# Threshold attention with a bilinear ffn: the transposes of a unit and the writes of its blocks moved behind the slot's first ffn portion

## The chip, the cores and the metric

The kernel runs on one core of a Trainium2 chip. The metric is the device time of one execution in microseconds (us), of which the median of three runs is given. All data is fp32 on the engines; the ffn weights come as 8-byte floats and are converted on the chip.

The engines are named as the profile names them: PE is TensorE (PEld its weight loads), DVE is VectorE, ACT is ScalarE, POOL is GpSimd, SP is SyncE, which here issues nearly all DMAs. Each engine works through its own queue in order; an instruction that waits holds all that stand behind it.

## What is computed

```python
# batch 8, heads 8, seq 576, head_dim 64; d_model 512, d_ff 1536
scores = scale * q @ k.T                       # for each batch and head
thresh = scores.max(-1) - tau
scores = where(scores >= thresh, scores, -1e9)
attn = exp(scores - scores.max(-1)); attn /= attn.sum(-1) + 1e-9
x = (attn @ v), heads side by side             # 4608 tokens x 512
out = ((x @ w_a) * (x @ w_b)) @ w_out
```

## The kernel before

**Units and slots.** Heads are taken in 32 pairs. The 576 query rows of a pair make four units of 128 rows and the 64 rows left over make, with those of the next pair, a fifth kind of unit; there are 144 units. The main loop (L1091) runs over slots g. In a slot a unit passes its first stage, and units before it pass later ones:

- `scores` (L389): PE multiplies q and k into two PSUM tiles of 128x576 (L404); DVE takes the row maxima (L411, two of them) and subtracts the threshold (L412, thr).
- `weigh` (L422): ACT forms the exponentials into a tile tw (L431, L432); DVE puts the threshold on them and sums the rows (L435, two of them). After that the score tiles are free.
- `reciprocal` and `normalise`: DVE inverts the sums (L446, L448) and ACT scales the tile tw (L454).
- one slot later, `turn_blocks` (L497): DVE transposes the blocks of 32x32 in both halves of tw, in place (L502, two instructions of 128x576), and four DMAs write tw to a swap block in DRAM (posted at L515). There are three tw buffers.
- two slots later, `turn_back` (L517): DMAs read the swap block back as wT, now turned as a whole. It comes at the start of the slot, or behind the pv product if the slot has one, since there are two wT buffers.
- three slots later, for the second unit of a half, `weighted` (L610): PE multiplies wT and v (pv, L546), ACT and DVE copy the result out of PSUM into x tiles (L553, L554).

The first nine slots (g up to 8) turn their units on PE instead. So 136 of the 144 units pass `turn_blocks`.

**The ffn between.** When four head pairs of a batch have delivered a block of 256 tokens, the block goes to the ffn, a generator that issues PE work in steps. `advance(cols)` (L998) runs it for so many columns. A slot gives the ffn its share of columns (`pace`) in four portions, 0.3, 0.35, 0.15 and 0.2 of it: the first behind the scores (L1131), the second behind `weigh` (L1156), then pv, then `normalise`, then the last two (L1198). What belongs to the steps is issued with them: PE's matmuls (L724 and L828 for the first layer, L894 for the second), and the evictions from PSUM, by ACT (L773 to L785, L834, L535) and by DVE: L777 and L794 add a product to another, L789, L798 and L836 multiply or add into h, L536 adds the second half of a result onto ACT's copy. All PSUM tiles, those of scores, pv and ffn, come from one pool of four.

**The order.** Program order is kept on each engine: `keep_order` (L41) chains the instructions of an engine as the Python code issued them. So the place of a call in the loop is the place of its instructions in the queues.

**The DMAs.** `post` (L139) issues a DMA at once up to slot 36. From slot 37 on it puts it on a list, `bulk`; writes of tw and reads of wT are put ahead of other entries of this and the last slot. `passed` (L169), called for each ffn step, takes entries off the list: one of 36864 elements, as each of the four writes of a unit is, for every 320 columns. Each entry also waits for the PE instruction issued last before it. `flush` issues what must be there now.

In a slot the part around the change reads, in order: overdue DMAs; `turn_back` of unit g-2 if no pv comes; `scores` of unit g; on DVE the two maxima and thr; then `turn_blocks` of unit g-1 and the first ffn portion; then the transposes of q tiles that are due (`prep`, L365); then `weigh` of unit g.

Of the kernel before, what the change touches and what calls it, by code (L numbers as in the profile page):

```python
# [23 lines left out]
BY_PE = 8  # L24
# [9 lines left out]
PORTIONS = (0.3, 0.35, 0.15, 0.2)  # L34
# [20 lines left out]
def kernel(  # L55
# [113 lines left out]
    def passed(columns):  # L169

        running["pump"] += columns
        while bulk and running["pump"] >= 0:
            running["pump"] -= PUMP * sum(math.prod(to.shape) for to, _ in bulk[0][2]) // PART
            pump()
        if not bulk:
            running["pump"] = min(running["pump"], 0)
# [320 lines left out]
    def turn_blocks(i, u):  # L497

        ws, _ = weights.pop((i, u))
        t = whole.pop((i, u))  # L500
        for w in ws:
            nc.vector.transpose(w, w)  # L502
        swap = scratch.tile([G, P, NSLOT * Q], FP32, tag="swap" if u < NT else "swapt", name="swap")
        swaps[i, u] = swap
        for g in range(G):
            if u < NT:
                moves = [(swap[g].rearrange("(r p) e -> p r e", p=Q),
                          t[g * Q:(g + 1) * Q].rearrange("p (r s) e -> p r (s e)", r=G))]
            else:
                moves = []  # L510
                for m in range(2):
                    j = g // 2 ^ m
                    moves.append((swap[2 * m + g % 2, j * D:(j + 1) * D].rearrange("(r p) e -> p r e", p=Q),
                                  t[g * Q:(g + 1) * Q, m * NB:(m + 1) * NB].rearrange("p (r s) e -> p r (s e)", r=2)))
            post(("tw", i, u), *moves)  # L515
# [63 lines left out]
    def exchange_blocks():  # L579
        while complete and not state["layer"] and not blocks:  # L580
            x, what = complete.pop(0)
            xs, done = ahead.pop(what[1:], (None, 0)) if what[0] == "half" else (None, 0)
            xs = xs or x_tile("xS")
            for hp in range(done, HP):
                exchange(x, xs, hp, 0, HALF, nc.gpsimd)
            blocks.append(((x, xs) + ((x_sums(x), x_sums(xs)) if state["first"] >= 3 * SEVENS else ()), what))
        if not state["layer"] and not blocks:
            for key, count in settled.items():
                xs, done = ahead.get(key) or (x_tile("xS"), 0)
                for hp in range(done, count):  # L590
                    exchange(x_of[key], xs, hp, 0, HALF, nc.gpsimd)
                ahead[key] = xs, count
# [80 lines left out]
    def first_sums(n, group):  # L673

        quarter = [w[:, NG - 1 - group].rearrange("p (z y e) w -> p z y (e w)", z=2, y=2)[:, :, y]
                   for w in (wa_sb, wb_sb) for y in range(2)]
        s1, s2, s4 = (sums_at(group, m).rearrange("p (z w) -> p z w", z=2) for m in range(3))
        a11, a12, a21, a22 = quarter
        out, a, b, op = ((s1, a21, a22, ALU.add), (s2, s1, a11, ALU.subtract), (s4, a12, s2, ALU.subtract),
                         (a21, a11, a21, ALU.subtract))[n]  # L680
        nc.gpsimd.tensor_tensor(out, a, b, op=op)
# [310 lines left out]
    def cost():  # L992

        return BLOCK_COLS - (NF // 2 * CH if state["sums"] else 0) - (SEVENS * 2 * HP * P if state["first"] >= 3 * SEVENS else 0)
# [3 lines left out]
    def advance(cols):  # L998
        running["owed"] += cols
        while running["owed"] > 0:  # L1000
            if running["ffn"] is None:
                exchange_blocks()
                if not blocks:
                    running["owed"] = 0.0
                    return
                if len(blocks[0][0]) == 4 and state["first"] == 3 * SEVENS:
                    for group in range(SEVENS):
                        first_sums(3, group)
                    state["first"] += 1
                if state["over"] and not state["all"]:  # L1010
                    first_sums(3, SEVENS)
                    state["all"] = True
                running["tiles"] = len(blocks[0][0])
                running["ffn"] = ffn(*blocks.pop(0))
                running["left"] = cost()
            step, rest, whole = next(running["ffn"], (None, 0, 0))
            if step == 0:
                running["owed"] = 0.0
                return
            if step is None:  # L1020
                running["ffn"] = None
                state["through"] += 1
            else:
                running["owed"] -= step
                running["left"] -= step
                passed(step)
                running["done"] = running["done"] + step if rest else 0
                running["rest"] = rest
                running["room"] = min(ROOM, whole // 2)
# [19 lines left out]
    def backlog():  # L1049
        return (len(blocks) + len(complete)) * cost() + (running["left"] if running["ffn"] is not None else 0)  # L1050
# [40 lines left out]
    for g in range(len(units) + PV_LAG):  # L1091
# [20 lines left out]
        pace = (PACE if g > BY_PE else PACE_EARLY) * BLOCK_COLS  # L1112
        if g > BY_PE:
            pace = min(pace, backlog() / (min([a for a in arrivals if a > g] + [len(units) + PV_LAG + 1]) - g))
# [10 lines left out]
        if g == 3:  # L1125
            for c in range(0, NSUM - TURNED - 2 * CW + 1, 2 * CW):
                extra.append(sums_u32[:, c:c + 2 * CW].rearrange("p (f w) -> p f w", w=2))
        if g > BY_PE and g <= len(units):
            turn_blocks(*units[g - 1])
        if g > BY_PE:  # L1130
            advance(PORTIONS[0] * pace)  # L1131
        for p in range(HP, NPR):
            for name, d in (("q0", 1), ("q1", 1)):
                if g == (second if name == "q1" else first)[p] - d - (name == "q1" and p % 2):
# [120 lines left out]
```

## Time and profile before

| what | value |
|---|---|
| time, median of 3 runs | 1418.59 us (1414.69, 1418.59, 1419.03) |
| the profiled execution, device time | 1420.35 us |
| its span, first to last instruction | 1418.6 us |
| mean granted TensorE clock | 0.994 |
| PE busy | 1369.6 us, 33980 matmuls |
| DVE busy | 1017.8 us, 2212 instructions |
| ACT busy | 678.8 us, 1245 instructions |
| POOL busy | 492.6 us, 675 instructions |
| DMA | 223.21 MB, 157 GB/s over the span |
| swap<-tw, issue to landing (median) | 3.0 us |
| wT<-swap, issue to landing (median) | 3.7 us |

Busy times are unions of the instructions that the profiler recorded on an engine. The ends of matmuls are modelled, since they are pipelined. A row of a group names line, engine, operation, out and in with shapes, the count; then total busy time and the mean of one; then the idle time of the engine just before these instructions and what ended it. In the list of waits, `A <- B: x, n, y` says that A waited for B x us in all, n times, y at most. In a timeline the first two columns are start and duration in us; in square brackets stands the idle time before, with its releaser.

### The profile page before, as it was taken

What the parts mean: (1) busy time and instruction counts of PE and PEld (TensorE: products, weight loads), DVE (VectorE), ACT (ScalarE), POOL (GpSimd) and SP (SyncE); (2) the same over time, 40 slices, a digit from 0 to 9 for tenths busy, and PEclk for the clock granted to TensorE, in tenths of its full rate; (3) what the DMA queues carried; (4) which work ended last, traced back from release to release, by engine and by line L of the source; (5) the groups of instructions that cost most, each with busy time, mean ns of one, the idle gap of its engine ahead of it and who ended that gap; (6) DMA issues with size and microseconds to landing.
All of it is one profiled execution on the core that took longest, in us unless ns stands there. A gap on an engine that the chain in (4) does not pass through costs nothing.

```text
span 1418.6 us, 76564 instructions
## 1 busy us (share of the span) xinstructions
PE 1369.6 (97%) x33980; PEld 1240.7 (87%) x33980; DVE 1017.8 (72%) x2212; ACT 678.8 (48%) x1245; POOL 492.6 (35%) x675
## 2 busy tenths in 40 slices
PE   6879999999999999999999999999999999999998
PEld 4778589999879897978998999998898899799998
DVE  6998877787777877775767777677767776745425
ACT  5986545545445455544444545454545455431110
POOL 2774442415060606051324233241515060608100
PEclk9999999999999999999999999999999999999999
DMA  9976875667656775666556775567555775550000
GB/s 213 238 225 193 204 207 161 168 167 204 169 128 181 189 194 153 171 163 173 137 137 152 183 182 165 131 162 206 163 146 143 200 188 156 133 152 18 4 19 18
DMA packets 327449, 223.21 MB, mean 157 GB/s; under 512 B 171600, under 2 KB 311632, under 8 KB 327120
## 3 DMA queue, kind: packets, MB, share of 16 engines
q1 hardware_dynamic: 323936, 216.95, 58.9%
q8 instruction: 267, 4.37, 1.3%
q10 hardware_dynamic: 3184, 1.38, 0.4%
q14 instruction: 62, 0.51, 0.1%
HBM read 128.58 MB, written 89.65 MB: 154 GB/s over the span
## 4 chain that ended last, share of the span: by engine, by line
PE 84%; DVE 8%; DMA 5%; issue 2%; SPq 1%; ACT 0%; DVEq 0%; ACTq 0%
PE pab L724 28%; PE po L894 20%; PE pab L828 15%; PE sc L404 10%; PE pv L546 9%; DVE mx L411 2%; DVE tw L502 2%; DMA vm<-in_v_dram 1%; DMA wT<-swap 1%; DVE tw L435 1%; PE po L964 1%; DVE low L311 1%; DMA qT<-in_q_dram 1%; DVE u L794 1%; DMA more_u<-in_moe_w_a_dram 0%
## 5 line engine op out<-in xcount | busy, mean ns | idle before, releaser
L411 DVE TENSOR_REDUCE mx<-sc 128x1 f32<-128x576 f32 x288 | 204.6, 751 | 131.5 <-PE sc L404 131.1
L454 ACT ACTIVATE tw<-tw,rcp 128x576 f32<-128x576 f32 x272 | 196.0, 768 | 203.6 <-DVE rcp L448 203.6
L686 POOL TENSOR_TENSOR h<-h,u 128x512 f32<-128x512 f32 x28 | 35.1, 1275 | 607.2 <-DVE h L798 429.0
L432 ACT ACTIVATE tw<-sc,bias,scalars 128x576 f32<-128x576 f32 x288 | 239.3, 831 | 10.9 <-PE pab L828 0.4
L435 DVE SCALAR_TENSOR_TENSOR tw<-sc,thr,tw 128x576 f32<-128x576 f32 x288 | 221.2, 798 | 9.6 <-ACT tw L432 9.0
L894 PE MATMUL po<-wo_sb,h 64*64 64x256 f32 (+1 forms) x3408 | 205.6, 367 | 1.2 <-DVE h L798 1.1
L502 DVE STREAM_TRANSPOSE tw<-tw 128x576 f32<-128x576 f32 x272 | 194.3, 752 | 0.8 <-ACT tw L454 0.8
L894 PEld LDWEIGHTS po<-wo_sb,h 64*64 64x64 f32 x3408 | 156.9, 133 | 26.6 <-DVE h L798 2.6
L404 PE MATMUL sc<-kT,qT 64*64 64x288 f32 x2016 | 168.9, 404 | 2.3 <-issue 0.6
L546 PE MATMUL pv<-wT,vm 64*64 64x128 f32 (+3 forms) x5040 | 165.5, 274 | 3.3 <-issue 2.4
L546 PEld LDWEIGHTS pv<-wT,vm 64*64 64x64 f32 x5040 | 154.1, 134 | 13.8 <-issue 8.0
L857 POOL TENSOR_TENSOR h<-h 128x256 f32<-128x256 f32 x168 | 117.3, 731 | 107.5 <-PE po L894 97.3
L894 PE MATMUL po<-sums_u,h 64*64 64x256 f32 x2448 | 153.5, 376 | 0.7 <-DVE h L836 0.7
L724 PE MATMUL pab<-xU,wb_sb 64*64 64x128 f32 x4352 | 137.7, 269 | 0.0
L724 PEld LDWEIGHTS pab<-xU,wb_sb 64*64 64x64 f32 x4352 | 133.0, 133 | 2.6 <-issue 0.9
L894 PEld LDWEIGHTS po<-sums_u,h 64*64 64x64 f32 x2448 | 116.3, 133 | 20.7 <-DVE h L836 1.1
L404 PEld LDWEIGHTS sc<-kT,qT 64*64 64x64 f32 x2016 | 104.0, 133 | 22.1 <-issue 6.1
L431 ACT ACTIVATE bias<-mx,scalars 128x1 f32<-128x1 f32 x288 | 82.7, 287 | 67.1 <-DVE mx L411 66.5
L553 ACT COPY xT<-pv 128x128 f32<-128x128 f32 (+1 forms) x68 | 17.6, 258 | 200.6 <-PE pv L546 200.6
L554 DVE COPY xT<-pv 64x128 f32<-64x128 f32 (+1 forms) x136 | 38.2, 281 | 91.2 <-PE pv L546 89.8
L724 PE MATMUL pab<-xS,wa_sb 64*64 64x128 f32 x2176 | 101.2, 269 | 1.7 <-issue 1.6
L535 ACT COPY kept<-po 128x512 f32<-128x512 f32 x65 | 34.8, 535 | 123.1 <-PE po L894 109.3
(159 smaller groups left out, 2428.1 us busy)
## 6 DMA issues: line engine op xcount, KB each, us to landing
wT<-swap SPq DMA_DIRECT2D x242, 288.0 KB, 3.7
swap<-tw SPq DMA_DIRECT2D x480, 144.0 KB, 3.0
vm<-in_v_dram SPq DMA_DIRECT2D x128, 72.0 KB, 2.5
swap<-tw SPq DMA_DIRECT2D x128, 72.0 KB, 3.0
kT<-in_k_dram SPq DMA_DIRECT2D x112, 72.0 KB, 3.4
wT<-swap SPq DMA_DIRECT2D x56, 144.0 KB, 3.5
out_dram<-kept SPq DMA_DIRECT2D x27, 256.0 KB, 3.9
qT<-in_q_dram SPq DMA_DIRECT2D x112, 40.0 KB, 2.8
```

The lines of the kernel that those rows point to most:

```text
L404: nc.tensor.matmul(sc[m][o * D:o * D + wide, c], qT[r, q0:q0 + wide], kT[r, c * SH:(c + 1) * SH], start=True, stop=True)
L411: nc.vector.tensor_reduce(mx[:, c], sc[j], axis=AX.XY, op=ALU.max)
L431: nc.scalar.activation(bias[:, j:j + 1], mx[:, j:j + 1], AF.Copy, scale=e_nscale)
L432: nc.scalar.activation(wb[j], sb[j], AF.Exp, bias=bias[:, j:j + 1], scale=e_scale)
L435: nc.vector.scalar_tensor_tensor(out=wv, in0=sb[j], scalar=thr[:, j:j + 1], in1=wv, op0=ALU.is_ge, op1=ALU.mult, accum_out=sums[:, j:j + 1])
L454: nc.scalar.activation(w, w, AF.Copy, scale=rcp[:, j:j + 1])
L502: nc.vector.transpose(w, w)
L546: nc.tensor.matmul(pv[c * D:(c + 1) * D, y], vm[rows, s], wT[y](rows, s), start=(s == 0), stop=(s == NSLOT - 1))
L724: nc.tensor.matmul(out[c * D:(c + 1) * D, r, f * P:(f + 1) * P], w[g][k][rows, w0:w0 + D], moving[k][rows], start=(fresh and k == 0 and f ...
L828: nc.tensor.matmul(pab[c:c + columns(), r], w[rows, f // n, k, fs + c:fs + c + columns()], moving, start=(k == 0), stop=(k == H - 1))
L857: (nc.vector if state["over"] else nc.gpsimd).tensor_tensor(*a, **kw)
L894: nc.tensor.matmul(po[c * D:(c + 1) * D, r, y, cut], ht[rows, t0:t0 + D], other[rows, f, cut], start=(f == 0), stop=(f == NF // 2 - 1))
```

## The change

The call of `turn_blocks` for the last unit moves from ahead of the first portion to behind it. The guard of each call is the same as before, and no instruction is added or taken away.

```diff
@@ -1125,10 +1125,10 @@
         if g == 3:
             for c in range(0, NSUM - TURNED - 2 * CW + 1, 2 * CW):
                 extra.append(sums_u32[:, c:c + 2 * CW].rearrange("p (f w) -> p f w", w=2))
+        if g > BY_PE:
+            advance(PORTIONS[0] * pace)
         if g > BY_PE and g <= len(units):
             turn_blocks(*units[g - 1])
-        if g > BY_PE:
-            advance(PORTIONS[0] * pace)
         for p in range(HP, NPR):
             for name, d in (("q0", 1), ("q1", 1)):
                 if g == (second if name == "q1" else first)[p] - d - (name == "q1" and p % 2):
```

On DVE the two L502 of a unit then stand behind the evictions of the first portion, if it has any, and ahead of L365 and L435 as before. The four writes come onto the list when the first portion has been issued, so `passed` can offer them from the second portion on; up to slot 36 they are issued at that place.

## Prediction

> **What bounds the kernel now.** I read the busy shares first, then the chain that ended last, then the groups of VectorE, then the list of waits of TensorE (PE), and last the timeline of single slots. A slot is one turn of the main loop; there are 144 units and 136 of them are transposed by VectorE (DVE), two instructions each.
>
> ```profile
> PE 1369.6 (97%) x33980; PEld 1240.7 (87%) x33980; DVE 1017.8 (72%) x2212; ACT 678.8 (48%) x1245; POOL 492.6 (35%) x675
> ...
> PE 84%; DVE 8%; DMA 5%; issue 2%; SPq 1%; ACT 0%; DVEq 0%; ACTq 0%
> ...
> L502 DVE STREAM_TRANSPOSE tw<-tw 128x576 f32<-128x576 f32 x272 | 194.3, 752 | 0.8 <-ACT tw L454 0.8
> ```
>
> PE is busy nearly throughout and is 84% of the chain, so a change on DVE can only win or lose what PE waits for DVE. The moved instructions are L502: 752 ns each, and over 272 of them DVE stood idle just 0.8 us before one. Their input is always there when their turn comes; they cost their own length to whatever is queued behind them. Today that is the evictions of the first ffn portion, in those slots that have any. The waits of PE say whether that hurts:
>
> ```profile
> PE pab L828 <- DVE h L836: 2.5, 1, 2.5
> ...
> PE pab L724 <- DVE u L794: 1.6, 5, 0.4
> ...
> PE po L894 <- DVE h L798: 1.1, 2, 0.5
> PE pab L724 <- DVE kept L536: 0.8, 3, 0.3
> PE pv L546 <- DVE h L836: 0.8, 1, 0.8
> ...
> PE po L894 <- DVE h L836: 0.7, 1, 0.7
> ...
> PE pab L828 <- DVE osb L536: 0.4, 1, 0.4
> ```
>
> The columns are total us, times, longest. These are 14 waits of 7.9 us for an eviction on DVE. I looked each up in the timeline, and in all 14 the eviction stands directly behind the two transposes. One of them, the slot at 457 us, on DVE:
>
> ```profile
> 458.80 0.23 DVE L412 TENSOR_SCALAR thr<-mx,scalars 128x2 f32<-128x2 f32 x1
> 458.93 1.43 DVE L502 STREAM_TRANSPOSE tw<-tw 128x576 f32<-128x576 f32 x2
> 460.29 1.18 DVE L798 TENSOR_TENSOR h<-h,pab 128x1024 f32<-128x1024 f32 x1
> 461.39 0.80 DVE L435 SCALAR_TENSOR_TENSOR tw<-sc,thr,tw 128x576 f32<-128x576 f32 x1
> ```
>
> and on PE:
>
> ```profile
> 456.98 0.44 PE L724 MATMUL pab<-xS,first_u 64*64 64x128 f32 x5
> ...
> 458.92 2.06 PE L828 MATMUL pab<-xS,wb_sb 64*64 64x256 f32 x32
> 461.53 1.31 PE L894 MATMUL po<-wo_sb,h 64*64 64x256 f32 x20 [0.55 <-DVE h L798]
> ```
>
> The product that L798 evicts was complete at 457.5, DVE was through with thr at 459.0, yet the eviction began at 460.29, after 1.36 us of transposes; PE ran dry at 460.98 and went on at 461.53.
>
> **The change, part by part.** Nothing is added or removed. Three things move.
>
> 1. The order on DVE. It differs only where an instruction of the first portion lies between L502 and L435. Going through DVE's timeline slot by slot I count 45 such slots of 136; in the other 91 DVE's queue is word for word the same. In the 45, an eviction (L536 0.67, L836 0.67, L789, L777, L798 1.2, two L794 1.35 us) starts up to 1.36 us sooner, and the transposes end later by its length. L435, behind both, starts at the same time as long as the eviction's data is ready when thr ends.
>
> Gain. Each of the 14 waits is shorter than 1.36 us and goes whole, except the first (2.54 us at 106.6: L502 began at 104.83, L836 at 106.19, so 1.4 of it). That is 7.9 - 2.5 + 1.4 = 6.8 us as the lower end. It is too small: the matmul before the wait is drawn with 0.27 to 0.38 us although such matmuls follow each other every 0.03 to 0.05 us, so PE could have begun the next group some 0.25 us before the drawn end. The weight loads, which run just ahead of the matmuls, show the same waits as 2.7 (1 time), 4.2 (6), 2.6 (3), 2.2 (3), 1.6 (2), 1.1 (1), 1.0 (2) and 0.9 (1), together 16.3 us in 19 waits; less 1.3 for the first that is 15.0, the upper end. I take 6.8 + 14 x 0.25 = 10.3 and round it down to 9, since a wait that goes now and then uncovers a smaller one behind it. [...]
>
> Cost. Where the data is not ready, DVE now waits with the transposes behind it instead of doing them meanwhile, and L435 starts later by that wait. From PE's and ACT's timeline I find 14 of the 45 slots: mostly L536, which needs ACT's copy L535 (0.59 us) after the last matmul of po, 0.4 to 1.0 us each; the largest is the slot at 645 us:
>
> ```profile
> 647.26 1.43 DVE L502 STREAM_TRANSPOSE tw<-tw 128x576 f32<-128x576 f32 x2
> 649.78 1.22 DVE L777 TENSOR_TENSOR h<-h,pab 128x1024 f32<-128x1024 f32 x1 [1.10 <-PE pab L724]
> 650.92 0.81 DVE L435 SCALAR_TENSOR_TENSOR tw<-sc,thr,tw 128x576 f32<-128x576 f32 x1
> ```
>
> There L435 moves to about 652.4. Over the 14 slots the delays add to about 9.6 us. Behind L435 wait the two PSUM tiles of the scores, the reciprocal and ACT's normalisation. In the window from 200 to 1260 us no wait of PE is put down to L435, and DVE still has 89.8 us of idle time in front of the pv copies (L554) and 131.1 in front of L411 later in the slots; that is the cover. Without it the price is 9.6 us. I take 1, nearer to nothing because the rows for it are empty there.
>
> 2. The four writes of the swap block. They are posted behind the first portion, so SP's list offers them one portion later, some 1280 columns by the code; the chain shows 224 matmuls of L724 in 6.11 us and four of them make 128 columns, so this is 1.1 us. They cannot start before the transposes end, 3.2 us after the scores; by then the next portion is running, so for the 91 slots their issue time hardly moves. In the list of SP's own waits:
>
> ```profile
> SPq L157 <- DVE tw L502: 107.5, 54, 6.5
> ```
>
> 54 times SP stood at such a write for the transposes, with everything behind it held. Now loads and stores that are already in the list go first; that can only bring q, k and v earlier (DVE waits 6.3 us for q today). In the 45 slots the write is later by the eviction, up to 1.35 us. Reader of the block: wT, one slot later, then pv another slot later. Setting the landings of the wT reads against the start of their pv matmuls, I find 2.1 us or more to spare everywhere after slot 36, mostly 5 to 9. Up to slot 36, where spare time sinks to 0.6 us at 174, nothing is held in the list and SP's order stays the same. Cost 0; without the cover, each of 64 pv pieces could wait up to 1 us.
>
> 3. The tile of three tw buffers. It is written again three slots later, so a write that is 1 to 2 us late holds nobody. Cost 0. In the last slot with a transpose (at 1256 us) the first portion has no DVE instruction, so the end is as before.
>
> Sum: -9 + 1 = -8 us. The profiled execution took 1420.35 us for a span of 1418.6; on the span the result is 1410.6. The three runs have a median of 1418.59, 1.8 below the profiled one, and the same 8 us off it give **1410.6, say 1411**.
>
> **Rivals.**
>
> *Hidden anyway.* PE is one engine in a long chain; if it arrives sooner it may just wait for the next thing, ACT's copies or the issue waits (4.4 and 2.4 us in that window, which no DVE order touches). For it: total idle time of PE after 200 us is small. Against: the 14 waits are separate, 40 to 150 us apart mostly, with gap-free PE work in between, so there is nothing to catch up with. A quarter to nothing of the gain would be left: 1416 to 1419. On this side stands the Trainium skill, page "Perfetto Trace Analysis", section "Matmuls": groups should rotate through PSUM banks so that an eviction overlaps the next group's matmuls. By that rule a late eviction costs nothing and the time stays at 1418.6; the 14 rows above speak against it here, for PE wants exactly the tile or the h block that is still being evicted.
>
> *Scores late (slower).* DVE waits in order at an eviction whose product PE has not finished, and L435, with the score tiles and the next unit's whole softmax behind it, pays. Price now: 9.6 us in 14 slots, if PE pays all of it; with the lower gain 6.8 that is +2.8. It decides once more than 11.1 us reach PE, since 11.1 - 6.8 = 4.3. At 25 unready slots of 0.7 us it is 17.5 - 6.8 = +10.7, 1429. For it: PE and DVE share these slots closely and PE's timing shifts. Against: a PE that is less held up finishes products sooner relative to DVE, and no wait for L435 is seen now.
>
> *Not what it says.* In two thirds of the slots the order does not change; if the 14 waits came by another way than the order, the time stays within 2 us. I count this with the first.
>
> **Chances.** A time is told from no change here when it differs by about 0.3%, 4.3 us. Forecast 0.70, all of it faster by more; hidden anyway and not what it says 0.18, within; scores late 0.12, slower. The likeliest case runs from 1418.6 - 15.0 = 1404 to 1414. The range goes on to 1421, so that it holds the hidden case and leaves out little more than the slower one and what is below.
>
> **What would show it.** Right: the seven rows above are gone from PE's waits or below 2 us in sum; the slot of the 457 us example shows L798 directly behind L412 and L502 behind L798; L435 begins at an unchanged distance from L411 in most slots; PE's busy time is the same and the span shorter by the waits. Wrong: new rows of PE waiting for L435 or for wT of more than 3 us in sum, L554 idle time turned into PE waits, or the seven rows gone and the span unchanged.

## Result and profile after

The kernel after takes 1409.42 us (median of 10 runs, 1403.65 to 1419.70); the kernel before, run beside it on the same chip, 1418.18 (10 runs, 1414.69 to 1423.33). The ratio is 0.9942, 95% interval [0.9919, 0.9965]: 8.8 us less, between 5.0 and 11.5 by the interval. The forecast was 1411.

The profiled execution took 1411.51 us for a span of 1409.7, 8.9 less than before. The page of the kernel after, in the rows shown of before:

```profile
PE 1363.7 (97%) x33980; PEld 1242.7 (88%) x33980; DVE 1019.9 (72%) x2212; ACT 678.2 (48%) x1245; POOL 492.8 (35%) x675
...
PE 88%; DVE 5%; DMA 3%; SPq 2%; issue 1%; ACT 1%; DVEq 0%; ACTq 0%
...
L502 DVE STREAM_TRANSPOSE tw<-tw 128x576 f32<-128x576 f32 x272 | 194.4, 752 | 0.8 <-ACT tw L454 0.8
```

The same instructions of the same length; DVE's share of the chain that ended last fell from 8% to 5%, and PE's grew. In the waits of PE (waited for: us in total, times, longest) this is left of the seven rows of before:

```profile
PE pab L828 <- DVE h L836: 1.2, 1, 1.2
...
PE po L894 <- DVE h L836: 0.8, 1, 0.8
...
PE pab L724 <- DVE kept L536: 0.6, 1, 0.6
```

14 waits of 7.9 us became 3 of 2.6. The first is the one at 106.6 us, which was 2.5. The other two are new places (1206 and 485 us). So the sign "below 2 us in sum" was missed by a little, by what came at new places. The slot of the example, now at 450 us, on DVE:

```profile
452.20 0.23 DVE L412 TENSOR_SCALAR thr<-mx,scalars 128x2 f32<-128x2 f32 x1
452.34 1.22 DVE L798 TENSOR_TENSOR h<-h,pab 128x1024 f32<-128x1024 f32 x1
453.47 1.43 DVE L502 STREAM_TRANSPOSE tw<-tw 128x576 f32<-128x576 f32 x2
454.82 0.78 DVE L435 SCALAR_TENSOR_TENSOR tw<-sc,thr,tw 128x576 f32<-128x576 f32 x1
```

and on PE, where the group that stood 0.55 us now follows without a gap:

```profile
452.45 1.50 PE L828 MATMUL pab<-xS,wb_sb 64*64 64x256 f32 x24
453.75 0.38 PE L894 MATMUL po<-wo_sb,h 64*64 64x256 f32 x1
```

Where the time goes can be read by windows. Each row gives PE's busy us and its matmuls in the window, then PEld, DVE, ACT, POOL, granted clock, DMA share, GB/s. Before, then after:

```profile
200.00:600.00 400.00, 395.25 (x9927) 360.05 (x9923) 301.51 (x666) 202.48 (x366) 125.54 (x185) 1.00 0.66 173
```

```profile
200.00:600.00 400.00, 397.91 (x10091) 358.77 (x10085) 306.92 (x677) 205.61 (x373) 125.51 (x185) 1.00 0.67 174
```

In the same 400 us PE does 164 matmuls more; at 400 / 9927 = 0.040 us each that is 6.6 us, at the same clock. Eight of the 14 waits lay in this window. Slot by slot (start of the first L411 of a slot, after minus before, us):

| slot | 11 | 23 | 32 | 45 | 55 | 77 | 96 | 143 |
|---|---|---|---|---|---|---|---|---|
| after - before | +1.9 | -2.2 | -3.8 | -4.7 | -7.4 | -10.7 | -8.7 | -8.0 |

The gain comes step by step between slots 11 and 77, where 13 of the 14 slots with a wait lie, and 2.7 us of it are given back later. The mean granted clock of the two profiled executions differs (0.994 and 0.999), but only ahead of 200 us (0.93 in the first 50 us and 0.98 up to 200 before, 1.00 after), and at slot 11 the kernel after was 1.9 us behind; the clock is not what made it faster. Only the step at slot 11 is mostly clock (0.88 to 0.91 from 100 to 130 us before): the kernel after needs 2.1 us less for this slot, and kernel 1 below, which keeps the wait there and had a clock of 1.000, 1.7 us less.

### The profile page after: what moved, and what is told of

The parts are those of the page before. It is cut to its first block, busy times and chain, and to the rows that moved or that the text cites. A ratio compares the mean times of both kernels' runs of the same rounds, so it can differ in the third digit from the quotient of the medians.

```text
span 1409.7 us, 76575 instructions
## 1 busy us (share of the span) xinstructions
PE 1363.7 (97%) x33980; PEld 1242.7 (88%) x33980; DVE 1019.9 (72%) x2212; ACT 678.2 (48%) x1245; POOL 492.8 (35%) x675
## 4 chain that ended last, share of the span: by engine, by line
PE 88%; DVE 5%; DMA 3%; SPq 2%; issue 1%; ACT 1%; DVEq 0%; ACTq 0%
PE pab L724 29%; PE po L894 21%; PE pab L828 18%; PE sc L404 10%; PE pv L546 9%; SPq L144 1%; DVE tw L435 1%; DVE mx L411 1%; DMA raw<-in_moe_w_b_dram 1%; DMA raw<-in_moe_w_a_dram 1%; DMA wT<-swap 1%; DVE low L311 1%; DVE tw L502 1%; DMA kT<-in_k_dram 0%; PE tp L483 0%
## 5 line engine op out<-in xcount | busy, mean ns | idle before, releaser
L411 DVE TENSOR_REDUCE mx<-sc 128x1 f32<-128x576 f32 x288 | 204.6, 751 | 119.3 <-PE sc L404 118.7
L432 ACT ACTIVATE tw<-sc,bias,scalars 128x576 f32<-128x576 f32 x288 | 239.4, 831 | 10.6 <-DMA qT<-in_q_dram 0.7
L435 DVE SCALAR_TENSOR_TENSOR tw<-sc,thr,tw 128x576 f32<-128x576 f32 x288 | 220.3, 796 | 9.9 <-ACT tw L432 9.8
L894 PE MATMUL po<-wo_sb,h 64*64 64x256 f32 (+1 forms) x3408 | 212.9, 367 | 0.0
L502 DVE STREAM_TRANSPOSE tw<-tw 128x576 f32<-128x576 f32 x272 | 194.4, 752 | 0.8 <-ACT tw L454 0.8
L894 PEld LDWEIGHTS po<-wo_sb,h 64*64 64x64 f32 x3408 | 169.7, 133 | 16.6
L404 PE MATMUL sc<-kT,qT 64*64 64x288 f32 x2016 | 176.1, 404 | 4.3 <-DVE xt L554 1.4
L894 PE MATMUL po<-sums_u,h 64*64 64x256 f32 x2448 | 157.8, 376 | 0.8 <-DVE h L836 0.8
L894 PEld LDWEIGHTS po<-sums_u,h 64*64 64x64 f32 x2448 | 125.4, 133 | 14.2 <-DVE h L836 1.3
L404 PEld LDWEIGHTS sc<-kT,qT 64*64 64x64 f32 x2016 | 107.1, 133 | 26.2 <-issue 6.8
L724 PE MATMUL pab<-xS,wa_sb 64*64 64x128 f32 x2176 | 107.7, 269 | 0.0
L554 DVE COPY xT<-pv 64x128 f32<-64x128 f32 (+1 forms) x136 | 38.1, 280 | 82.2 <-PE pv L546 80.6
```

What stands on the lines that cost most here:

```text
L404: nc.tensor.matmul(sc[m][o * D:o * D + wide, c], qT[r, q0:q0 + wide], kT[r, c * SH:(c + 1) * SH], start=True, stop=True)
L411: nc.vector.tensor_reduce(mx[:, c], sc[j], axis=AX.XY, op=ALU.max)
L432: nc.scalar.activation(wb[j], sb[j], AF.Exp, bias=bias[:, j:j + 1], scale=e_scale)
L435: nc.vector.scalar_tensor_tensor(out=wv, in0=sb[j], scalar=thr[:, j:j + 1], in1=wv, op0=ALU.is_ge, op1=ALU.mult, accum_out=sums[:, j:j + 1])
L724: nc.tensor.matmul(out[c * D:(c + 1) * D, r, f * P:(f + 1) * P], w[g][k][rows, w0:w0 + D], moving[k][rows], start=(fresh and k == 0 and f ...
L894: nc.tensor.matmul(po[c * D:(c + 1) * D, r, y, cut], ht[rows, t0:t0 + D], other[rows, f, cut], start=(f == 0), stop=(f == NF // 2 - 1))
```

## Experiments

All kernels were timed against the kernel before on the same chip; the ratios are to it. On these chips the kernel before took 1422.9 to 1424.3 us, some 5 more than in the result, so the times expected of kernels 1 to 6, 8 and 9 are to be read as ratios to 1418: 1409 is 0.9935, 1415 is 0.998. The theory: PE gains the 14 waits because the evictions no longer stand behind the transposes. The rivals: the gain comes from SP's queue (the later writes), or from DVE's order in other slots. Each diff is against the kernel before, unless it says otherwise.

**1. Only the writes later.** The transposes stay; the loop over the four writes goes to a function of its own, called behind the portion.

```diff
-    def turn_blocks(i, u):
+    def turn_only(i, u):
...
+    def write_blocks(i, u):
+        t = whole.pop((i, u))
...
         if g > BY_PE and g <= len(units):
-            turn_blocks(*units[g - 1])
+            turn_only(*units[g - 1])
         if g > BY_PE:
             advance(PORTIONS[0] * pace)
+        if g > BY_PE and g <= len(units):
+            write_blocks(*units[g - 1])
```

> The transposes stay ahead of the first ffn portion; only the four writes of the swap block are posted behind it, so DVE's queue is that of before and SP's queue that of the changed kernel. Theory (the gain comes from DVE's evictions, which no longer stand behind the transposes): no gain, 1418 within 3 us, and the seven rows of PE waiting for an eviction on DVE stay at 7 to 9 us. Rival (the gain comes from SP: loads and stores go ahead of writes that wait for the transposes): 1409 within 3 us.

Ratio 0.9990 [0.9975, 1.0005], 1421.15 us: no gain that can be told from nothing, and by the interval 3.6 us at most. PE's waits for these evictions stay, 7.5 us in sum; two of the rows from 200 to 1260 us (line numbers are 3 higher in this kernel; L797 is L794, L801 is L798):

```profile
PE pab L727 <- DVE u L797: 1.4, 4, 0.4
PE po L897 <- DVE h L801: 1.1, 2, 0.5
```

The gain does not come from SP's queue.

**2. Only the 45 slots whose DVE order differs, and 3. only the 14 slots with a wait.**

```diff
+        late = g in (11, 21, 22, 30, 35, 44, 48, 53, 54, 62, 66, 71, 72, 121)
-        if g > BY_PE and g <= len(units):
+        if g > BY_PE and g <= len(units) and not late:
             turn_blocks(*units[g - 1])
         if g > BY_PE:
             advance(PORTIONS[0] * pace)
+        if g > BY_PE and g <= len(units) and late:
+            turn_blocks(*units[g - 1])
```

(with a list of 45 in kernel 2).

> The call moves only in the 45 slots whose first portion has a DVE instruction; in the other 91 the writes are posted where they were. DVE's queue is that of the changed kernel. Theory: the whole gain, 1409 within 3 us. Rival (SP's order in all slots): about a third of it, 1415 or more.

> The call moves only in the 14 slots in which the profile before shows PE waiting for an eviction behind the transposes. Theory in its narrow form (these 14 waits are the gain): the whole gain, 1409 to 1411. Rival (many small delays in all 45 slots, which the waits do not show, add up): about a third, 1414 to 1416.

1414.89 us, 0.9950 [0.9929, 0.9971], and 1415.11 us, 0.9946 [0.9926, 0.9965]: both have the whole gain, as far as the intervals can tell, and the rivals' third of it (about 0.998) lies outside both. In kernel 3 none of the seven rows is left from 200 us on. So a tenth of the change is all of it, and the effect sits in those 14 slots.

**4. All but the 14 "unready" slots**, where DVE was expected to stand at an eviction whose data is late, **and 5. the kernel after once more** beside it. Kernel 4 is kernel 3 with another list:

```diff
+        late = g not in (38, 39, 56, 57, 74, 75, 76, 85, 89, 98, 102, 114, 115, 132)
```

> The call moves in all slots but the 14 in which the profile before says that the eviction is not ready when thr ends. The prediction put the cost of these 14 at 1 us of 9.6 possible. By that, 1408 within 3 us, the same as the changed kernel. If PE pays for the later L435 there: 1400 to 1404.

> The changed kernel once more, on the chip and beside the runs that it is compared with here: 1409 within 3 us, for the three kernels above and against the scatter from chip to chip.

1414.73 us, 0.9940 [0.9917, 0.9963], and 1416.44, 0.9948 [0.9929, 0.9968]. The 14 unready slots cost 0.0008, 1.1 us, with an uncertainty of some 4: not told from nothing. The kernel after itself gained 7.4 us here, where the result had 8.8.

**6. The transposes further back**, behind the two L435.

```diff
-        if g > BY_PE and g <= len(units):
-            turn_blocks(*units[g - 1])
         if g > BY_PE:
             advance(PORTIONS[0] * pace)
...
         if here:
             weigh(i, u)
+        if g > BY_PE and g <= len(units):
+            turn_blocks(*units[g - 1])
```

> The transposes go one step further back, behind the two L435 of the slot; evictions of the first portion stand as in the changed kernel, and the score tiles come free up to 1.4 us sooner in all 136 slots. Theory (what PE waited for were the evictions, and it hardly ever waits for L435): no further gain, 1409 within 3 us, with less spare time for wT. Rival (any DVE work that releases PSUM gains when it stands ahead of the transposes): as much again or more, 1400 or less. If the turned blocks come too late, PE waits for wT and the time is 1412 or more.

1446.61 us, 1.0161 [1.0136, 1.0186]: 23 us slower, far from the theory and its rival. Late wT, the third case, is not the reason: PE waits 3.6 us for it, in 3 waits. DVE's waits in this kernel:

```profile
DVE tw L435 <- ACT tw L432: 62.0, 156, 2.7
...
DVE qT L365 <- DMA qT<-in_q_dram: 33.0, 10, 4.6
```

The first was 9.8 us in 19 waits in the kernel after, the second 7.0 in 7. The transposes filled the time in which ACT forms the exponentials (L432); without them DVE stands there, and they come in front of the reciprocal instead. From slot 37 to 142, L435 begins 3.06 us after the first L411 in the mean (3.72 in the kernel after), but the reciprocal L448 7.82 us after it (7.24), and a slot lasts 9.07 us (8.79). Which of these makes the 23 us, the unfilled time, the late reciprocal or the late q, this kernel does not tell.

**7. The transposes behind the softmax**, to tell the late reciprocal from the unfilled gap: as 6, but behind `normalise`.

> The two transposes and the four writes stand at the end of the slot's softmax, behind the reciprocals (L448) and ACT's normalisation, no longer ahead of L435. Question: why did transposes behind L435 cost 23 us. If because the reciprocal, the pv copies (L554) and the second portion's evictions stood behind them, this kernel wins most of it back, 1412 to 1425. If because DVE has nothing else to do while ACT forms the exponentials, and its work just lies later, the loss stays, 1435 or more. A third way: the writes come some 4 us later and wT is late for pv, which would show as rows of PE pv L546 waiting for DMA of more than 10 us.

1448.57 us, 1.0180 [1.0149, 1.0212]. The reciprocal now comes at 6.90 us, but the third way came true. PE's waits:

```profile
PE pv L546 <- DMA wT<-swap: 18.6, 10, 4.9
```

So this kernel doesn't decide between the two (DVE's wait for L432 is 40.8 us here); what it shows is that the writes bear no delay of that size.

**8 and 9. More delay, ahead of and behind the portion.** The order of after, and in all slots two more row maxima of the scores, 0.71 us of DVE's busy time each, into a spare tile (the diff is against the kernel after).

```diff
+        if here and g > BY_PE:
+            spare = small.tile([P, 2], FP32, tag="spare", name="spare")
+            for j, s in enumerate(scored[i, u][0]):
+                nc.vector.tensor_reduce(spare[:, j:j + 1], s, axis=AX.XY, op=ALU.max)
         if g > BY_PE:
             advance(PORTIONS[0] * pace)
```

(in 9 behind `advance`).

> The changed kernel with two extra row maxima of the scores (750 ns each, into a tile that nobody reads) in 135 slots, ahead of the first portion, where the transposes stood. Theory (a delay of 1.5 us ahead of the evictions is what cost the time, whatever makes it): the 9 us come back, and the kernel is 6 to 14 us slower than the same with the extra maxima behind the portion. Rival (it was the transposes or their writes themselves): both extra kernels take the same time within 3 us.

> The same two extra row maxima, but behind the first portion and ahead of the transposes: evictions as early as in the changed kernel, L435 1.5 us later in all slots. Theory: cheap, since PE does not wait for L435: 1409 to 1414. Rival (DVE's load or a late L435 bounds): 1418 or more, as with the maxima ahead of the portion.

1475.82 us, 1.0375 [1.0353, 1.0398], and 1481.69, 1.0416 [1.0392, 1.0439]. They are 53 and 59 us slower than before, and their order is the opposite of the expected one. Two reasons are in the traces. L435 is later by 1.1 to 1.2 us in the mean of the slots (4.82 and 4.91 us behind L411), over 135 slots instead of 14. And ACT was held up by the new reader of the scores: in kernel 8, from ACT's waits,

```profile
ACT tw L432 <- DVE spare L1131: 44.1, 29, 2.8
```

and 57.3 us in kernel 9, so the dose was not clean.

**10 and 11. The dose in the 14 slots alone**, with maxima of the last unit's tw, which ACT doesn't wait for.

```diff
+        if g in (11, 21, 22, 30, 35, 44, 48, 53, 54, 62, 66, 71, 72, 121):
+            spare = small.tile([P, 2], FP32, tag="spare", name="spare")
+            last = whole[units[g - 1]]
+            for j in range(2):
+                nc.vector.tensor_reduce(spare[:, j:j + 1], last[:, j * NB:(j + 1) * NB], axis=AX.XY, op=ALU.max)
         if g > BY_PE:
             advance(PORTIONS[0] * pace)
+        if g > BY_PE and g <= len(units):
+            turn_blocks(*units[g - 1])
```

(in 11 the maxima stand behind `advance`; the call ahead of it is gone in both).

> The kernel before, with two row maxima of the last unit's tile tw (128x576 each, about 0.65 us each, into a spare tile that nobody reads) put ahead of the first portion in the 14 slots alone where PE was seen to wait (11, 21, 22, 30, 35, 44, 48, 53, 54, 62, 66, 71, 72, 121); the transposes stand behind the portion in all slots, as after the change. The maxima are extra work and do not touch the result. Theory (what stands ahead of the first evictions is paid by PE in these slots, 14 x about 0.6 us): the gain of the change is lost again, 1416 to 1421 us where the kernel before has about 1422, and the rows of PE waiting for L794, L798 and L836 come back. Rival (the gain came from elsewhere, such as the loads on SP's queue): 1411 to 1415, as after the change.

> The same two maxima in the same 14 slots, now behind the first portion and ahead of the transposes. L435 and all behind it are later by 1.3 us in these slots, as in the kernel with the maxima ahead. Theory: the evictions stay early, the rows stay away; what is left is the lateness of L435, by the rate seen with maxima in all slots (0.43 us a slot) 14 x 0.4 = 6 us at most, so 1413 to 1420, and 3 to 8 us below the kernel with the maxima ahead. Rival (PE pays for DVE's load wherever it stands): the two are within 2 us of each other.

1426.99 us, 1.0017 [0.9996, 1.0038], and 1423.30, 0.9998 [0.9979, 1.0017]; the difference is 3.7 us (0.3 to 6.9 when the 12 runs of each are drawn anew). With the maxima ahead, the rows are back, 7.8 us in sum (7.9 before the change):

```profile
PE pab L828 <- DVE h L836: 2.5, 1, 2.5
...
PE po L894 <- DVE h L836: 1.6, 2, 0.9
...
PE pab L724 <- DVE u L794: 1.4, 4, 0.4
PE pab L724 <- DVE kept L536: 1.2, 3, 0.6
...
PE po L894 <- DVE h L798: 1.1, 2, 0.5
```

With the same maxima behind they stay away, and another row comes:

```profile
PE pv L546 <- DVE tw L435: 1.7, 2, 0.9
```

The theory holds for the rows and for the sign; the interval of the difference also takes in the rival's 2 us, and both medians lie above what was expected (0.996 to 0.999 for 10 and 0.994 to 0.999 for 11, of a kernel before at 1422). But the maxima behind the portion, which reach only L435 (later by 14.7 us in these 14 slots together), took the gain as well. Of three orders in 14 slots, against the kernel after: evictions late (before) about 8 us, L435 late (11) about 8, both (10) about 10. The two do not add up.

The timelines show why. In slot 44 of kernel 11, PE stood before the product of pv until the slot's first L435 was through:

```profile
376.31 0.09 DVE L435 DVE_READ_ACCUMULATOR tw<-sc,thr,tw 128x1 f32 x1
376.50 2.21 PE L546 MATMUL pv<-wT,vm 64*64 64x128 f32 x69 [0.76 <-issue]
```

In five of the 14 slots (11, 44, 54, 62 and 72) a group of PE starts 0.05 to 0.10 us after the first L435 ends, after idle times of 1.32, 0.76, 0.87, 0.54 and 0.87 us. For slots 11, 54 and 72 the profile names L435 as what ended the wait; for 44 and 62 it says "issue", and L435 is inferred from the times. L435 frees a score tile, and all PSUM tiles come from one pool of four. Before the change pv started 1.10 to 1.12 us behind the end of that L435 in slots 44, 54, 62 and 72; in the kernel after it is 0.06 to 0.50 us. The gain has used up this slack. In kernel 10 PE is already held up by the eviction in these four slots, and then stands only 0.10 to 0.13 us before pv. So slot 44 lasts 9.90 us in both kernels (8.79 in the kernel after): one delay hides the other.

**12. An earlier reciprocal.** On top of the change (the diff is against the kernel after) the transposes of q tiles (L365) go from ahead of L435 to behind the reciprocals.

```diff
-        for p in range(HP, NPR):
-            for name, d in (("q0", 1), ("q1", 1)):
-                if g == (second if name == "q1" else first)[p] - d - (name == "q1" and p % 2):
-                    prep(p, name)
...
             reciprocal(i, u, nc.scalar if converting else nc.vector)
             normalise(i, u)
+        for p in range(HP, NPR):
+            for name, d in (("q0", 1), ("q1", 1)):
+                if g == (second if name == "q1" else first)[p] - d - (name == "q1" and p % 2):
+                    prep(p, name)
```

> After the change, and in addition the transposes of the q tiles that are due for the next slot (L365, 47 of them between slot 37 and the end, 0.36 us each, with 7.0 us of waits for the load of q) stand behind the reciprocals (L448) instead of ahead of L435. Theory (what PE pays is how late the softmax of a unit ends on DVE: over slots 37 to 142, in the kernels run so far, the mean time from L411 to L448 and the length of a slot go up together, about 0.5 us of slot for 1 us): L448 is sooner by up to 47 x 0.36 + 7 = 24 us in sum, so 5 to 12 us below the kernel after, a ratio to the kernel before of 0.986 to 0.991. Rival 1 (a reciprocal that comes sooner than today brings nothing; only lateness costs): 0.993 to 0.996, as after the change. Rival 2 (qT is late for the next scores): rows of PE sc L404 waiting for DVE qT L365 of over 5 us, ratio 0.996 or more.

1422.19 us, 0.9993 [0.9975, 1.0011]: the time of before is back, the theory of this run fell. The reciprocal was sooner (7.09 us instead of 7.24), the slot longer (8.87). PE's waits have a row for the late qT, smaller than the rival asked for:

```profile
PE sc L404 <- DVE qT L365: 2.4, 4, 1.2
```

What took the rest of some 6 us is open, but not its place: in the profiled execution the 14 slots are 8.4 us shorter than before, as with the change alone, and 7.2 us more than in the kernel after lie in the 56 slots that have a transpose of q. No kernel here is faster than the kernel after beyond the noise.

## Why the prediction was right, and where not

**The gain: right.** It was put at 9 between 6.8 and 15.0, less 1 of cost; gain and cost together came to 8.8 (5.0 to 11.5). Kernel 3 shows that it comes from those 14 slots, kernel 1 that it is DVE's order and not SP's, kernel 10 that putting other work of the same length there brings the waits back. The slots themselves show it without the scatter of whole runs. The table gives for six of the 14 by how many us a slot is shorter than before, from its first L411 to that of the next slot (minus means longer):

| slot | 35 | 44 | 48 | 54 | 72 | 121 |
|---|---|---|---|---|---|---|
| the wait before | 0.41 | 0.41 | 0.28 | 0.55 | 0.55 | 0.68 |
| kernel after, and kernels 2 to 5 (to 0.01) | 0.66 | 0.64 | 0.51 | 0.80 | 0.80 | 0.92 |
| kernel 1, writes only | 0.00 | 0.00 | -0.05 | 0.00 | 0.00 | -0.01 |
| kernel 10, evictions and L435 late | 0.01 | -0.47 | -0.01 | -0.33 | -0.33 | 0.00 |
| kernel 11, only L435 late | 0.43 | -0.47 | 0.10 | -0.33 | -0.33 | 0.92 |

Each of these slots wins its wait and 0.23 to 0.25 us more, the correction of 0.25 that the prediction took from the drawn ends. In other slots of the 14, such as 53 and 71, the executions differ by up to 1.7 us. All 14 together are 9.5 us shorter in the kernel after, 8.1 in kernel 3 and 6.2 in kernel 5; all other slots from 9 on together 0.4, -0.3 and 0.1. In kernel 1 the 14 come to 2.0, of which 1.7 is slot 11 and its clock, as said above. That the total came within 1 us of the forecast is partly luck: 10.3 was rounded down to 9 without a row for it, and kernel 5 gained 7.4. One reading was wrong, without effect: the 14 waits lie 9 to 77 us apart (the last 447), not 40 to 150.

The weight loads' 15.0 lies outside the interval, the 6.8 of the matmul row inside. The Trainium skill (page "Perfetto Trace Analysis", section "Identifying the Most-Contended Engine") prefers the busy share of the weight loads to that of the matmuls for telling how close TensorE is to its roofline; it does not speak of single waits, and here the weight loads' row was too long for them. The "Matmuls" section of the same page of the Trainium skill asks that groups rotate through PSUM banks, so that an eviction overlaps the next group's matmuls; read as the prediction reads it, the time would not have changed. Kernel 3 speaks against that reading with 7.7 us in 14 slots (0.54% of 1423).

**The cost of late scores: the size right, the reason too generous.** In the traces L435 of the 14 unready slots is later by 9.3 us together (58.1 us behind L411 before, 67.4 after); the forecast was 9.6. The waits of DVE for ACT's copy grew as said (`kept L536` from 30.7 to 38.3 us). That the sums agree is partly luck. In the slot that was to be the worst, at 645 us, now at 637, L435 came sooner instead of 1.5 us later (4.84 us behind L411, 5.26 before), since its product was ready sooner; the other 13 were later by 9.7 us together instead of some 8:

```profile
638.99 1.22 DVE L777 TENSOR_TENSOR h<-h,pab 128x1024 f32<-128x1024 f32 x1 [0.66 <-PE pab L724]
640.13 1.43 DVE L502 STREAM_TRANSPOSE tw<-tw 128x576 f32<-128x576 f32 x2
641.48 0.78 DVE L435 SCALAR_TENSOR_TENSOR tw<-sc,thr,tw 128x576 f32<-128x576 f32 x1
```

PE paid 1.1 us of it within some 4 (kernels 4 and 5), as the 1 taken. But the ground given, that idle time in front of L554 and L411 covers L435, is not a general one: kernel 11 made L435 later by 14.7 us and paid about 8. The traces point to how soon PE needs the tile that L435 frees. In five slots of kernel 11 PE stood at it, as shown above; these are 5.6 of the 8.9 us by which the 14 are longer there than in the kernel after, and the rest is open. Of the 14 unready slots eight have a pv, and in the kernel after it starts in six of these before the first L435 ends, so it does not need that tile; in none of the 14 does a wait of PE end with L435. So the low cost belongs to these slots, which the prediction did not look up. In the 14 slots with a wait L435 did not move (64.4 and 63.6 us), as forecast.

**The SP step: not borne out, harmless in the sum.** "That can only bring q, k and v earlier" does not show. DVE waits for q and k 9.0 us before (6.3 and 2.7) and 11.9 after:

```profile
DVE qT L365 <- DMA qT<-in_q_dram: 7.0, 7, 1.8
...
DVE kT L365 <- DMA kT<-in_k_dram: 4.9, 3, 2.1
```

Kernel 5, the same program, has 9.5 and kernel 1 has 11.0, so neither sooner nor later can be told from the scatter. SP stands as long at the writes as before (111.2 us in 49 waits for L502, 107.5 in 54), so nothing shows that others went first. "2.1 us or more to spare everywhere" for wT did not stay either: at 471 us it is 0.5 us, at 957 us 1.4. No wait of PE came of it after slot 36.

**PE's busy time was to be the same**; it fell by 5.9 us, and only 3.0 of the 8.9 us of span are idle time less. Part of it may go with the clock: kernel 1, with the waits and a clock of 1.000, had 1367.9 us instead of 1369.6 at 0.994. For the rest the likely reason is the drawn end: the last matmul before a wait is drawn 0.27 to 0.38 us long instead of 0.03 to 0.05, so each vanished wait takes some 0.25 us of drawn work with it, as the slots above show, by this estimate 3.5 us for 14. The busy time itself does not settle it: the profiled executions with the change have 1363.7 to 1371.7 us, the last in kernel 3 at a clock of 0.995.

**Rivals.** Hidden anyway and not what it says are out by kernels 1 to 3; scores late did not decide, but kernel 11 shows that it would have taken the gain, had the evictions made L435 late in the slots of the gain.

## What to carry over

On an engine that works in order, look up which instruction another engine stands at, and see what is queued directly ahead of it: work with slack belongs behind it. Move it no further than that without a look at what it will stand in front of next, and whether it fills a gap of its own: the same transposes one step further back cost 23 us instead of gaining 9. Before counting a delay as free, look up who next takes what the delayed instruction frees, and how soon. A wait list of a few us in a few slots can be the whole effect; try the move in those slots alone to know.

## What the runs showed of the hardware

- The busy time of the weight loads is no steady measure: the kernel after had 1242.7 us in one profiled execution and 1271.6 in another (spans 1409.7 and 1412.4), kernel 12 1297.7.
- The visible waits of the matmul row were too short: six slots won 0.23 to 0.25 us more than the wait that went.
- Where the softmax is late on DVE in all slots, a slot is longer by about half as much: L448 later by 0.58 us went with 0.28 us (kernel 6), 0.80 us with 0.39 (kernel 8), 0.84 us with 0.41 (kernel 9). That the one causes all of the other is not shown. The other way round it did not hold: L448 sooner by 0.15 us went with slots longer by 0.08 (kernel 12).
- A DVE maximum over 128x576 took 0.71 us of busy time from PSUM (190.9 us for 270, kernel 8) and 0.70 us from SBUF (19.7 us for 28, kernel 10).
